# An attention + MLP block on one core: the MLP of the last chunk as its own pipeline (TensorE transposes, residual summed beforehand, w1 in two row halves, w3 in two row ranges, Newton rstd)

## The chip, the cores and the metric

The kernel runs on one core of a Trainium2 chip. The metric is device time in microseconds (us), the median of several executions.

Engine names in the profile: PE = TensorE matmul, PEld = TensorE weight load, DVE = VectorE, ACT = ScalarE, POOL = GpSimd, SPq = the DMA queue fed by SyncE.

A second measure, the **tail**: from the end of the last eviction of an attention output (the last `f_On<-f_O,f_rl`) to the end of the span, both read from the timeline of one profile. The change acts almost only there.

## The reference, cut to what matters

```python
# x: 2048 x 640; 32 heads of 128; keys and values 2048 long; w3: 640 x 1728, w4: 1728 x 640
mod = silu(c) @ w_mod                      # sa, ca, ga, sb, cb, gb: six vectors of 640
h = layernorm(x) * (1 + ca) + sa
x = x + ga * (attention(h) @ wo)           # LayerNorm without weights, eps 1e-5
h = layernorm(x) * (1 + cb) + sb
# MLP B(h):
g  = gelu(layernorm(h) @ w1)               # 640 columns in four groups of 160;
gs = shift rows of the groups by +1, -1, +2, -2
x1 = h + gs @ w2
B  = x1 + gelu(layernorm(x1) @ w3) @ w4
x = x + gb * B
```

The row shift matters: row r of `gs` needs rows r-2 to r+2 of `g`. So the MLP of the last tile of a chunk has to wait for the next chunk, and the last chunk has five tiles of 128 rows for w2, w3 and w4 instead of four.

## The kernel before: the parts that the change touches

The queries are done in four chunks of 512 rows (`NC` = 4). While attention of one chunk runs, the MLP of the chunk before it (`phase_b`) is slipped in between. The last chunk's MLP has nothing to hide behind. A small scheduler orders the operations of each engine by the priority that is the last argument of `P.op`; it then puts in semaphores for the data.

```python
    def ln(src, src_tiles, prio):                       # LayerNorm statistics and rstd
        ...                                             # 2 x bn_stats, bn_aggr on DVE
        P.op("ACT", lambda e: e.activation(rs[i].ap, mv[i][:, 1:2], ACT.Ln, bias=EPS), ...)
        P.op("ACT", lambda e: e.activation(rs[i].ap, rs[i].ap, ACT.Exp, scale=-0.5), ...)
        return mv[i], rs[i]

    def back_to_exp(g, prio):                           # EXPSET = "natural_log_exp_and_others"
        o = P.op("ACT", lambda e: e.preload_act_table_set(EXPSET), ..., after=tuple(g))
        return (o,)

    def phase_b(ch):
        last = ch == NC - 1
        ...                                             # weights w1, w2 (and once w3) by DMA
        for i in range(4):                              # residual, two LayerNorms, DMA transpose
            w = y_t * ga ; a = w + x                    # 2 DVE operations of 128x640
            mvt, rst = ln(a) ; b = modulated(a, ...)
            mvt, rst = ln(b) ; nr = (b - mean) * rstd
            dma("SP", e.dma_start_transpose(nT_t[:, :, i * 128:(i + 1) * 128], nr.ap), ...)
        for n in range(KT):                             # w1: 5 groups, each over all 512 rows
            ...matmul 128x512, then gelu into us_t, shifted by one or two columns...
        if not last:
            gate[X1 + 1, 0] = back_to_exp(g1, X1 - 2)
        for t in tl:                                    # w2: 4 tiles, in the last chunk 5
            ...matmul in two column halves, DVE adds each half into b...
            mvt, rst = ln(b) ; nr = (b - mean) * rstd   # second LayerNorm of the MLP
            dma("SP", e.dma_start_transpose(nT_t[...], nr.ap), ...)
        for f in range(NF):                             # w3: 14 groups, in the last chunk over
            for (r0, r1) in ranges:                     # two ranges of 320 rows; each reads ALL tiles
                P.op("PE", mm, KT * MM(n), (WB,) + tuple(nT[t - t0] for t in tl), (m,), ...)
                ...gelu...
        for t in tl:                                    # w4 and the output
            ...matmul in two halves; DVE: + b per half, * gb, + a; DMA out...
```

(Bodies are shortened to their arithmetic; `...` marks cuts.) Note two things: every w3 group waits for the transposes of all five tiles, and `back_to_exp`, which puts a table set with both Ln and Exp back after the gelus, is left out in the last chunk.

## Time and profile before

| | before |
|---|---|
| time, median (3 runs) | 1488.18 us (1486.7 to 1490.71) |
| span of the profiled execution | 1482.6 us |
| PE busy over the span | 94% |
| tail | 115.1 us |
| table loads on ScalarE in the tail | 12 |

The page of the kernel before: busy time and share, and the chain that ended last.

```profile
PE 1399.9 (94%) x13043; PEld 926.6 (62%) x13043; DVE 568.5 (38%) x1330; ACT 1104.1 (74%) x1292; POOL 6.2 (0%) x14
...
PE 90%; ACT 4%; DVE 3%; DMA 1%; issue 1%; SPq 0%; DVEq 0%
```

For most of the span PE is the limit, and the change does nothing about that. The busy table of the kernel before, by stretches of 20 us, shows where it is not. Columns: stretch, its length, then busy us of PE, PEld, DVE, ACT and POOL with instruction counts, the granted TensorE clock, the DMA share and GB/s.

```profile
1380.00:1400.00 20.00, 0.25 (x1) 0.13 (x2) 16.68 (x36) 4.12 (x15) 0.00 (x0) 0.50 0.15 33
1400.00:1420.00 20.00, 15.18 (x75) 6.61 (x73) 8.23 (x21) 13.35 (x20) 0.00 (x0) 0.93 0.21 57
1420.00:1440.00 20.00, 9.56 (x59) 5.68 (x60) 3.67 (x9) 12.75 (x22) 0.00 (x0) 0.74 0.25 68
1440.00:1460.00 20.00, 19.48 (x137) 11.81 (x136) 3.04 (x5) 7.60 (x18) 0.00 (x0) 1.00 0.03 9
```

PE stands almost still in 1380 to 1400 (0.25 us busy) and does half its time in 1420 to 1440. The timeline of the kernel before says why. Columns: start, duration, engine, line, operation, `out<-in`, and in brackets the idle time before it and what ended that.

```profile
1399.75 4.94 PE L578 MATMUL f_M<-f_nT,f_WA 128*128 128x512 bf16 x15 [23.38 <-DMA f_nT<-f_nrm]
...
1415.88 0.20 ACT L360 ACTIVATE f_rs<-f_mv 128x1 f32<-128x1 f32 x1 [0.29 <-DVE f_mv L359]
1416.10 1.28 ACT L361 ACT_TABLE_LOAD   x1
...
1417.40 0.20 ACT L361 ACTIVATE f_rs<-f_rs 128x1 f32<-128x1 f32 x1
1417.62 1.28 ACT L360 ACT_TABLE_LOAD   x1
1417.63 0.61 DVE L605 TENSOR_SCALAR f_nrm<-f_xb,f_mv,f_rs 128x640 bf16<-128x640 f32 x1 [0.98 <-ACT f_rs L361]
...
1427.35 0.61 DVE L605 TENSOR_SCALAR f_nrm<-f_xb,f_mv,f_rs 128x640 bf16<-128x640 f32 x1 [2.37 <-ACT f_rs L361]
...
1430.44 9.81 PE L625 MATMUL f_M<-f_nT,f_WB 128*128 128x320 bf16 x59 [10.49 <-DMA f_nT<-f_nrm]
```

w1 (L578) starts only when four tiles have been through two LayerNorms and a DMA transpose; PE had waited 23.4 us. w2's tiles then cost "Ln, table load, Exp, table load" each, 3.3 us from one normalised tile to the next, and w3 (L625) starts when the fifth is normalised and transposed: 62.9 us into the tail. From there PE is the limit: w3 21.1 us, w4 21.2 us.

### The profile page before, as it was taken

The page shows a single profiled execution, that of the slowest core. Times are in us where ns is not written, and L with a number is a line of the kernel's source. Part 1 is how long each engine was busy: PE and PEld are TensorE (multiplying, and loading weights), DVE is VectorE, ACT ScalarE, POOL GpSimd, SP SyncE. Part 2 cuts the span into 40 slices and gives each one's busy share as a digit, 9 for nine tenths or more (in the row PEclk, how much of TensorE's full clock was granted, in tenths as well). Part 3 has the DMA queues.
Part 4 walks back from the last instruction along what each step waited for, and adds up shares of the span by engine and source line. Part 5 has one row for each costly group of instructions (what it writes and reads, how often), then busy time and mean ns, then how long its engine had stood idle before and what let it go on. Part 6 is the DMA issues. An engine that isn't in the chain of part 4 may idle for free.

```text
span 1482.6 us, 30158 instructions
## 1 busy us (share of the span) xinstructions
PE 1399.9 (94%) x13043; PEld 926.6 (62%) x13043; DVE 568.5 (38%) x1330; ACT 1104.1 (74%) x1292; POOL 6.2 (0%) x14
## 2 busy tenths in 40 slices
PE   6999999999999999999999999999999999999367
PEld 3666666666666666666666566666666666666134
DVE  5332333335552135224653125322833224323633
ACT  4868888888898776788888675788888685786261
POOL 0000000000000000000000000000000000000000
PEclk8999999999999999999999999999999999999689
DMA  7997899999899478998988466988998765985020
GB/s 185 214 220 129 159 173 181 191 206 181 174 174 179 103 127 188 196 177 159 188 169 173 106 132 140 216 167 172 177 184 168 136 126 115 197 165 114 22 67 25
DMA packets 755788, 232.60 MB, mean 157 GB/s; under 512 B 716608, under 2 KB 755008, under 8 KB 755648
## 3 DMA queue, kind: packets, MB, share of 16 engines
q1 hardware_dynamic: 755648, 230.60, 78.4%
q8 instruction: 104, 1.70, 0.5%
q14 instruction: 36, 0.29, 0.1%
HBM read 136.82 MB, written 2.62 MB: 94 GB/s over the span
## 4 chain that ended last, share of the span: by engine, by line
PE 90%; ACT 4%; DVE 3%; DMA 1%; issue 1%; SPq 0%; DVEq 0%
PE f_O L475 31%; PE f_S L462 28%; PE f_M L450 9%; PE f_M L507 9%; PE f_M L646 4%; PE f_M L625 4%; ACT f_PT L465 3%; PE f_M L578 1%; PE f_M L598 1%; DVE f_st L357 1%; PE f_M L333 1%; DMA f_KTs<-in_A_k_cache_dram 1%; ACT L361 0%; DMA f_nT<-f_nrm 0%; DMA f_WA<-in_w_mod_dram 0%
## 5 line engine op out<-in xcount | busy, mean ns | idle before, releaser
L465 ACT ACTIVATE f_PT<-f_S 128x1024 bf16<-128x1024 f32 x1024 | 998.4, 1025 | 237.7 <-PE f_O L475 125.5
L475 PEld LDWEIGHTS f_O<-f_V,f_PT 128*128 128x128 bf16 x8192 | 547.6, 98 | 223.2 <-DVE f_On L486 18.9
L475 PE MATMUL f_O<-f_V,f_PT 128*128 128x129 bf16 x8192 | 640.5, 220 | 1.4 <-DVE f_On L486 0.9
L462 PE MATMUL f_S<-f_QT,f_KTs 128*128 128x512 bf16 x2048 | 603.5, 379 | 12.5 <-ACT f_PT L465 11.3
L453 DVE CAST f_QT<-f_M 128x512 bf16<-128x512 f32 x128 | 88.5, 691 | 486.0 <-PE f_M L450 485.9
L450 PE MATMUL f_M<-f_hT,f_wq 128*128 128x512 bf16 x640 | 228.6, 382 | 0.8 <-ACT f_hT L399 0.8
L462 PEld LDWEIGHTS f_S<-f_QT,f_KTs 128*128 128x128 bf16 x2048 | 165.8, 97 | 79.6 <-ACT f_PT L465 36.1
L507 PE MATMUL f_M<-f_wo,f_OT 128*128 128x320 bf16 x1024 | 179.2, 301 | 0.9 <-DVE f_yacc L515 0.8
L515 DVE TENSOR_TENSOR f_yacc<-f_M,f_yacc 128x320 f32<-128x320 f32 x224 | 109.5, 490 | 144.2 <-PE f_M L507 143.4
L507 PEld LDWEIGHTS f_M<-f_wo,f_OT 128*128 128x128 bf16 x1024 | 94.0, 98 | 61.0 <-DVE f_yacc L515 6.1
L486 DVE TENSOR_TENSOR f_On<-f_O,f_rl 128x256 bf16<-128x256 f32 x256 | 107.9, 422 | 6.6
L484 DVE RECIPROCAL f_rl<-f_O 128x2 f32<-128x2 f32 x256 | 43.4, 170 | 141.6 <-PE f_O L475 137.0
L450 PEld LDWEIGHTS f_M<-f_hT,f_wq 128*128 128x128 bf16 x640 | 62.0, 98 | 44.4 <-issue 2.2
L646 PE MATMUL f_M<-f_WA,f_gT 128*128 128x320 bf16 x448 | 79.6, 300 | 0.6 <-ACT f_gT L629 0.5
L625 PE MATMUL f_M<-f_nT,f_WB 128*128 128x512 bf16 (+5 forms) x350 | 65.9, 343 | 12.2 <-DMA f_nT<-f_nrm 10.5
L629 ACT ACTIVATE f_gT<-f_M 128x512 bf16<-128x512 f32 (+3 forms) x70 | 35.8, 511 | 39.5 <-PE f_M L625 39.4
L625 PEld LDWEIGHTS f_M<-f_nT,f_WB 128*128 128x128 bf16 (+1 forms) x350 | 31.8, 100 | 41.8 <-DMA f_nT<-f_nrm 10.8
L646 PEld LDWEIGHTS f_M<-f_WA,f_gT 128*128 128x128 bf16 x448 | 40.2, 97 | 24.8 <-issue 7.7
L578 PE MATMUL f_M<-f_nT,f_WA 128*128 128x512 bf16 x100 | 25.6, 398 | 24.7 <-DMA f_nT<-f_nrm 23.4
L360 ACT ACTIVATE f_rs<-f_mv 128x1 f32<-128x1 f32 x64 | 12.8, 203 | 41.0 <-DVE f_mv L359 40.9
L650 DVE TENSOR_TENSOR f_tmp<-f_M,f_xb 128x320 f32<-128x320 f32 x32 | 15.7, 491 | 65.9 <-PE f_M L646 65.6
L578 PEld LDWEIGHTS f_M<-f_nT,f_WA 128*128 128x128 bf16 x100 | 9.3, 101 | 36.8 <-DMA f_nT<-f_nrm 23.7
(75 smaller groups left out, 378.9 us busy)
## 6 DMA issues: line engine op xcount, KB each, us to landing
f_V<-in_A_v_cache_dram SPq DMA_DIRECT2D x128, 512.0 KB, 5.0
f_wq<-in_A_wq_dram SPq DMA_DIRECT2D x128, 160.0 KB, 2.9
f_wo<-in_A_wo_dram SPq DMA_DIRECT2D x32, 640.0 KB, 5.0
f_WA<-in_B_w_dram SPq DMA_DIRECT2D x40, 160.0 KB, 2.9
f_WA<-in_B_w_dram SPq DMA_DIRECT2D x8, 800.0 KB, 5.1
f_xin<-in_A_x_dram SPq DMA_DIRECT2D x32, 160.0 KB, 3.6
out_dram<-f_ob SPq DMA_DIRECT2D x16, 160.0 KB, 4.0
f_WA<-in_w_mod_dram SPq DMA_DIRECT2D x3, 800.0 KB, 5.3
```

The lines of the kernel that those rows point to most:

```text
L450: P.op("PE", lambda e, kk=kk: e.matmul(m.ap, w[:, kk, :], hT_t[ch % 2][:, kk, :], start=(kk == 0), stop=(kk == KT - 1)), MM(QC), (w,) + tu ...
L453: P.op("DVE", lambda e: e.tensor_copy(q.ap, m.ap), dve(QC, True), (m,), (q,), s - 4)
L462: ins = e.matmul(sp[:, r * QC:(r + 1) * QC], k[:, kt * 128:(kt + 1) * 128], q.ap, start=True, stop=True)
L465: last_exp[s, j] = P.op("ACT", lambda e, sp=sp, pt=pt: e.activation(pt.ap.rearrange("p k q -> p (k q)"), sp.ap, ACT.Exp, scale=SCALE), 104 ...
L475: ins = e.matmul(o[b][:, u * 129:u * 129 + 129], pt[:, r, qt * 128:(qt + 1) * 128], v[:, kt, 0:129], start=(kt == 0 and u == 0), stop=(kt ...
L484: P.op("DVE", lambda e, ov=ov, i0=i0: e.reciprocal(rl_t[:, i0:i0 + 2].unsqueeze(2), ov[:, 0:258].rearrange("p (u d) -> p u d", u=2)[:, :, ...
L486: P.op("DVE", lambda e, ov=ov, i0=i0, b=b: e.tensor_tensor(out=On_t[gs][:, 2 * b:2 * b + 2, hh, :], in0=ov[:, 0:258].rearrange("p (u d) -> ...
L507: ins = e.matmul(m[:, 0:HD], OT_t[gs][:, qt, hh, :], w[:, hh, sl], start=(hh == 0), stop=(hh == HG - 1))
L515: P.op("DVE", lambda e, m=m, qt=qt, sl=sl: e.tensor_tensor(out=y_t[:, qt, sl], in0=m[:, 0:HD], in1=y_t[:, qt, sl], op=ALU.add), dve(HD, Tr ...
L578: ins = e.matmul(m.ap, w1v[:, kk, n * 128:(n + 1) * 128], nT_t[:, kk, 0:QC], start=(kk == 0), stop=(kk == KT - 1))
L625: ins = e.matmul(m[0:fs[f], 0:n], w3v[:, kk, f * 128:f * 128 + fs[f]], nT_t[:, kk, r0:r1], start=(kk == 0), stop=(kk == KT - 1))
L646: ins = e.matmul(m[:, 0:HD], gT_t[0:fs[f], f, i * 128:(i + 1) * 128], w4v[0:fs[f], f, sl], start=(f == 0), stop=(f == NF - 1))
```

## The change

The intent: give the last chunk its own code, in which each stage starts on the first tiles as soon as they are there, and take waiting and detours out of the chain. In short:

- the last `wo` group goes straight from PSUM to the residual, on TensorE-transposed attention outputs; ga times the sum of the earlier groups, plus x, is formed on GpSimd beforehand (`tail_front`);
- the `wo` matmuls of the last but one group pulled closer together (priority steps of 0.2 instead of 0.5; not in the cut below), so that their sum is ready for that;
- all transposes of the tail on TensorE, copied out of PSUM by ScalarE;
- w1 in two halves of 256 rows, w3 in two row ranges (tiles 0 and 1, tiles 2 to 4), each waiting only for its own tiles;
- the rstd of the second LayerNorm by three Newton steps (seed on VectorE, nine GpSimd operations of 128x1) instead of Ln and Exp, so that no table load is needed there;
- gb times b plus x1 formed on GpSimd while w3 runs, so the output needs two VectorE operations per tile instead of four.

```diff
-        if not last:
-            gate[X1 + 1, 0] = back_to_exp(g1, X1 - 2)
+        gate[X1 + 1, 0] = back_to_exp(g1, X1 - 2)
 ...
+    def pe_transpose(src, n, reads, dst, dst_t, prio):      # n PE transposes into one PSUM tile,
+        ...                                                 # then one ScalarE copy
+    def rstd_newton(v, i, prio):
+        r, q = rs[i], nw[i]
+        P.op("DVE", ... q0 = var + EPS)
+        P.op("DVE", ... r = q0 as int >> 1)
+        P.op("DVE", ... r = 0x5f3759df - r, as int)
+        for _ in range(3):
+            P.op("POOL", ... q1 = r * r * q0)               # tensor_scalar, 128x1
+            P.op("POOL", ... q1 = 1.5 - 0.5 * q1)           # tensor_scalar, 128x1
+            P.op("POOL", ... r = r * q1)                    # tensor_tensor, 128x1
+    def tail_front(ch):                                     # queued 4 heads before the end
+        for i in range(4):
+            P.op("POOL", ... y = y * ga) ; P.op("POOL", ... y = y + x)
+    def tail(ch):
+        for i in range(4):
+            pe_transpose(On...) ; wo: 8 matmuls
+            P.op("DVE", ... v = wo * ga) ; P.op("DVE", ... a = v + y)
+            mvt, rst = ln(a) ; modulated(...) ; mvt, rst = ln(b) ; nr = ...   # Ln and Exp as before
+            pe_transpose(nr...)
+        for hv in range(2):                                 # w1, rows 0-255, then 256-511
+            ...matmul 128x256 needs nT[2*hv], nT[2*hv+1]; gelu...
+        for i in range(5):                                  # w2
+            ...matmul; P.op("DVE", ... b = w2 + b); bn; rstd_newton; nr = ...; pe_transpose(nr...)
+            P.op("POOL", ... b = b * gb, priority pr + 5)
+            P.op("POOL", ... b = b + a,  priority pr + 5)
+        for i0, i1 in ((0, 2), (2, 5)):                     # w3 over tiles 0-1, then tiles 2-4
+            for f in range(NF):
+                ...matmul needs nT[i0:i1] alone; gelu...
+        for i in range(5):                                  # w4
+            ...P.op("DVE", ... v = w4 * gb) ; P.op("DVE", ... o = v + b) ; DMA out
 ...
-        phase_b(ch)
+        if ch < NC - 1:
+            phase_b(ch)
+        else:
+            tail(ch)
```

(The added arithmetic is written as formulas. In the list of added lines `i` is the tile.)

## The prediction

> **What bounds it now.** The page: span 1482.6 us, PE busy 94%; the chain of waits is 90% PE. That holds until attention ends near 1367 us. The last chunk's MLP then runs alone, and the busy table by stretches shows it: PE is busy 0.25 us of 1380–1400, 15.2 of 1400–1420, 9.6 of 1420–1440, 19.5 of 1440–1460. So the tail, about 115 us, is bounded by stages in turn (timeline): 1367–1397 VectorE (residual, two LayerNorms, four tiles); 1397–1399.7 a DMA transpose; 1400–1408.6 w1; 1408.7–1430.4 w2 with five times "Ln, table load, Exp, table load" (3.3 us a tile, each load 1.28) and another DMA transpose (2.4 us in the chain); 1430.4–1473.2 w3 and w4, PE-bound (21.1 us each); then output. Before 1367 nothing is on offer.
>
> **What the change does.** The order of instructions before the last two wo groups is unchanged. In the tail:
> - Removed: 8 VectorE adds of wo into yacc (0.49 us each, 3.9), most DMA transposes (2.4 us each; PE 0.7 cold plus ScalarE copy 0.69 instead), two table loads of twelve, Ln/Exp of the second LayerNorm.
> - Added: Newton rstd, 3 VectorE and 9 GpSimd operations on 128x1 per tile. The trace has no such GpSimd operation; I estimate 0.2 us each (its 128x32 memset is 0.13), so 3.6 us for two interleaved tiles. GpSimd also takes 128x640 f32 multiply and add. The Trainium skill, "GPSIMD Engine Reference", section 3.1, gives 4497 ns for a 2048-element tensor_tensor; scaled, an estimate of 1.4 us. No run here shows it yet.
> - Moved: w1 in two halves. But in ScalarE's new order the Ln/Exp pairs of tiles 2 and 3 sit between the gelus of half 0: three times load, Ln, load, Exp, load (about 4.3 us each, 13 in all). VectorE's normalisation of tiles 2 and 3 waits for them. The skill, "ScalarE: Activation LUTs", section "What ACT_TABLE_LOAD costs", says about 1283 ns a load; the trace agrees (1283), without the further drain.
>
> **Sum, walked by hand with the trace's durations.** Tiles 0 and 1 normalised at 1383; half 0 of w1 gelu'd at 1401, not 1391, because of the table loads; half 1 at 1411.7 (before: all of w1 at 1408.6, so this stage loses 3 us). w2, Newton and transposes overlap it, so w3's first range starts near 1417.5 instead of 1430.4: 13 us gained. From there PE is nearly continuous: 256-column groups paced by the two PSUM banks (0.6 us each, 14), 2 inserted transposes 1.5, w4 4.2 us a tile, 384-column groups 0.82 each: PE ends near 1460.5 instead of 1473.2. The last output saves 0.5 (no half add). Gain 13 us, 0.9%.
>
> **Prediction: 1475 us, range 1466 to 1482** (8 in 10). Faster by over 2%: 3%; within 2%: 96%; slower by over 2%: 1%.
>
> **What would show it right.** Timeline: w1's gelus stretched over 1386–1412 with about ten table loads among them; VectorE idle 3 to 10 us for ScalarE's rstd of tiles 2 and 3; first w3 matmul at 1415–1420; then PE over 90% busy; start of tail within 1 us of 1367.
>
> **What would make it wrong.** GpSimd's small operations at 0.4 us or its 640-wide ones at 2.5: PE would stall at the transposes of the last three tiles, and 5 to 9 us go back. A first w3 matmul before 1412 would mean the table loads hid better than I think: 1466 or less. Cold PE clock through w3: 2 us more.

## The result, and the profile after

| | before | after |
|---|---|---|
| time, median (4 runs each, same rounds) | 1487.44 us (1485.82 to 1490.71) | 1478.95 us (1478.29 to 1479.21) |
| ratio | | 0.994, 95% interval 0.9922 to 0.9957 |
| span of the profiled execution | 1482.6 | 1477.0 |
| tail | 115.1 | 104.2 |
| first w3 matmul, us into the tail | 62.9 | 50.0 |
| table loads in the tail | 12 | 10 |

A ratio is the mean time of one kernel's fast runs over that of the other's fast runs of the same rounds, so it is not quite the ratio of the medians. The verdict is "same" at 2%, as predicted: 0.6% faster, where the prediction had 0.9%.

**Two profiles cannot be laid over each other by absolute time.** These are the last attention evictions of before and of after, from which the tail is counted:

```profile
1367.10 0.42 DVE L486 TENSOR_TENSOR f_On<-f_O,f_rl 128x256 bf16<-128x256 f32 x1
```

```profile
1372.36 0.42 DVE L490 TENSOR_TENSOR f_On<-f_O,f_rl 128x256 bf16<-128x256 f32 x1
```

After's tail starts 5.3 us later. Of that, 4.4 us were already there at head 124 of 128, before the first instruction that differs, and they had built up over the whole span. It is noise of the execution: over the profiles of after and of its eleven variants, all of which leave this prefix alone, the start of head 124 lies anywhere from 1321.0 to 1327.9 us, with the same instructions before it (but for matmul records missing from some traces). From head 124 to the last eviction, however, it is 46.6 us in all of them and 45.8 us in before, 0.84 us less. The likely cause is the wo matmuls that were pulled together: in after, head 126, in which they now stand, takes 2.7 us longer, and head 127 takes 1.8 less. No run undoes this part alone. So the reproducible gain is 10.8 us of tail (115.06 less 104.23) less 0.8, which is 10.0 us; the medians show 8.5.

The busy table of the kernel after, same columns (its tail starts at 1372.8):

```profile
1380.00:1400.00 20.00, 5.67 (x28) 3.02 (x29) 15.51 (x33) 10.63 (x22) 0.00 (x0) 0.55 0.00 0
1400.00:1420.00 20.00, 13.71 (x89) 8.21 (x87) 7.24 (x19) 15.16 (x25) 5.40 (x19) 0.76 0.14 40
1420.00:1440.00 20.00, 16.51 (x133) 11.12 (x134) 9.53 (x27) 7.70 (x18) 17.77 (x36) 1.00 0.14 44
1440.00:1460.00 20.00, 19.42 (x123) 11.09 (x120) 2.96 (x3) 7.12 (x15) 2.49 (x2) 1.00 0.05 17
```

In 1420 to 1440 PE now does 16.5 us instead of 9.6, and GpSimd, idle in the tail before, is busy 17.8 of 20 us. The timeline of the kernel after, in two places:

```profile
1394.34 1.28 ACT L364 ACT_TABLE_LOAD   x1
...
1395.64 0.20 ACT L364 ACTIVATE f_rs<-f_mv 128x1 f32<-128x1 f32 x1
1395.86 1.28 ACT L365 ACT_TABLE_LOAD   x1
1397.15 0.20 ACT L365 ACTIVATE f_rs<-f_rs 128x1 f32<-128x1 f32 x1
1397.37 1.28 ACT L752 ACT_TABLE_LOAD   x1
1397.46 0.89 DVE L383 SCALAR_TENSOR_TENSOR f_xb<-f_tmp,f_rs,f_mod 128x640 f32<-128x640 f32 x1 [3.82 <-ACT f_rs L365]
...
1418.78 1.54 POOL L780 TENSOR_TENSOR f_xb<-f_xb,f_mod 128x640 f32<-128x640 f32 x1
1418.87 1.80 DVE L776 TENSOR_SCALAR f_nrm<-f_xb,f_mv,f_rs 128x640 bf16<-128x640 f32 x1 [0.80 <-POOL f_rs L697]
...
1422.83 5.49 PE L790 MATMUL f_M<-f_nT,f_WB 128*128 128x256 bf16 x45
...
1429.13 0.44 PE L677 MATMUL f_M<-f_ident,f_nrm 128*128 128x128 bf16 x5 [0.81 <-DVE f_nw L687]
```

First, the table loads: in the middle of w1's gelus stands load, Ln, load, Exp, load, 4.3 us, for one rstd of tile 2, and VectorE waits 3.8 us for it (L383). Second, from 1418 on GpSimd paces: the normalisation at 1418.87 took 1.80 us where the same operation takes 0.61, beside a GpSimd operation of 1.54; and the transposes that w3's first range has to let through (L677) wait for VectorE. The chain that ended last, in order of time, of the kernel after:

```profile
1418.87 1.82 DVE f_nrm L776
...
1420.75 1.55 POOL f_xb L780
1422.30 2.72 POOL f_xb L781 x2
...
1433.48 1.49 POOL f_xb L780
1434.97 0.15 POOL f_rs L697
1435.12 1.36 POOL f_xb L781
```

The small Newton result (L697, 0.15 us) stands in GpSimd's queue between residual operations of 1.4 to 1.5 us each (L780, L781), and the chain runs through both.

The tail's sum closes: w3 starts 12.9 us sooner (62.9 to 50.0); from there to the end of w4 it takes 45.7 us instead of 42.8, so 2.9 are lost; the output after the last matmul is 0.9 shorter (8.5 instead of 9.4). 12.9 - 2.9 + 0.9 = 10.9, but for rounding the 10.8 above.

### The profile page after: what moved, and what is told of

Read it like the earlier page. It is cut to its first block, busy times and chain, and to the rows that moved or that the text cites. A ratio compares the mean times of both kernels' runs of the same rounds, so it can differ in the third digit from the quotient of the medians.

```text
span 1477.0 us, 30150 instructions
## 1 busy us (share of the span) xinstructions
PE 1393.4 (94%) x12903; PEld 933.0 (63%) x13129; DVE 563.7 (38%) x1322; ACT 1109.9 (75%) x1302; POOL 43.3 (3%) x77
## 4 chain that ended last, share of the span: by engine, by line
PE 84%; ACT 6%; DMA 3%; DVE 3%; issue 2%; POOL 1%; SPq 1%
PE f_O L479 30%; PE f_S L466 27%; PE f_M L514 9%; PE f_M L454 8%; ACT f_PT L469 4%; PE f_M L661 3%; PE f_M L641 3%; DMA f_KTs<-in_A_k_cache_dram 2%; PE f_S L807 1%; PE f_M L620 1%; PE f_M L601 1%; DMA f_V<-in_A_v_cache_dram 1%; PE f_M L790 1%; PE f_M L333 1%; DVE f_st L356 0%
## 5 line engine op out<-in xcount | busy, mean ns | idle before, releaser
L466 PE MATMUL f_S<-f_QT,f_KTs 128*128 128x512 bf16 x1876 | 566.6, 379 | 26.1 <-ACT f_PT L469 13.7
L454 PE MATMUL f_M<-f_hT,f_wq 128*128 128x512 bf16 x592 | 210.5, 382 | 0.9 <-ACT f_hT L403 0.8
L514 PE MATMUL f_M<-f_wo,f_OT 128*128 128x320 bf16 x992 | 173.0, 299 | 0.2
L661 PE MATMUL f_M<-f_WA,f_gT 128*128 128x320 bf16 (+1 forms) x308 | 58.4, 299 | 0.2
L641 PE MATMUL f_M<-f_nT,f_WB 128*128 128x512 bf16 (+3 forms) x208 | 44.7, 362 | 2.0 <-ACT f_gT L645 1.7
L645 ACT ACTIVATE f_gT<-f_M 128x512 bf16<-128x512 f32 (+3 forms) x42 | 23.6, 562 | 28.2 <-PE f_M L641 28.2
L661 PEld LDWEIGHTS f_M<-f_WA,f_gT 128*128 128x128 bf16 (+1 forms) x308 | 27.4, 97 | 15.9 <-issue 5.1
L641 PEld LDWEIGHTS f_M<-f_nT,f_WB 128*128 128x128 bf16 (+1 forms) x210 | 19.3, 98 | 22.7 <-ACT f_gT L645 5.6
L356 DVE BATCH_NORM_STATS2 f_st<-f_xb 128x6 f32<-128x320 f32 x64 | 29.9, 484 | 0.4
L605 ACT ACTIVATE f_us<-f_M 32x512 bf16<-32x512 f32 (+3 forms) x27 | 16.0, 594 | 9.3 <-PE f_M L601 9.1
L665 DVE TENSOR_TENSOR f_tmp<-f_M,f_xb 128x320 f32<-128x320 f32 x22 | 10.8, 492 | 31.6 <-PE f_M L661 31.3
```

Of the source, the lines that this page charges most:

```text
L356: P.op("DVE", lambda e, hf=hf: e.bn_stats(st[i][:, hf * 6:hf * 6 + 6], src[:, hf * HD:(hf + 1) * HD]), dve(HD), src_tiles, (st[i],), prio)
L454: P.op("PE", lambda e, kk=kk: e.matmul(m.ap, w[:, kk, :], hT_t[ch % 2][:, kk, :], start=(kk == 0), stop=(kk == KT - 1)), MM(QC), (w,) + tu ...
L466: ins = e.matmul(sp[:, r * QC:(r + 1) * QC], k[:, kt * 128:(kt + 1) * 128], q.ap, start=True, stop=True)
L514: ins = e.matmul(m[:, 0:HD], OT_t[gs][:, qt, hh, :], w[:, hh, sl], start=(hh == 0), stop=(hh == HG - 1))
L641: ins = e.matmul(m[0:fs[f], 0:n], w3v[:, kk, f * 128:f * 128 + fs[f]], nT_t[:, kk, r0:r1], start=(kk == 0), stop=(kk == KT - 1))
L661: ins = e.matmul(m[:, 0:HD], gT_t[0:fs[f], f, i * 128:(i + 1) * 128], w4v[0:fs[f], f, sl], start=(f == 0), stop=(f == NF - 1))
```

## The experiments

Each kernel is the changed kernel (in one case the kernel before) with the edit shown. All results were correct. For each: what was expected, and what it gave. Rows with the same letter under "chip" ran on the same chip beside the same runs of before.

| kernel | chip | time, us (median) | ratio to before | tail | w3 starts | w4 starts | last tile normalised | table loads |
|---|---|---|---|---|---|---|---|---|
| before | | | 1 | 115.1 | 62.9 | 84.5 | 60.4 | 12 |
| after | | 1478.95 | 0.994 | 104.2 | 50.0 | 61.9 | 66.2 | 10 |
| e1: w1 whole | a | 1481.97 | 0.9958 | 106.9 | 52.0 | 66.2 | 64.0 | 1 |
| e2: gelus behind the last Exp | a | 1481.29 | 0.9957 | 106.2 | 51.5 | 65.3 | 62.5 | 1 |
| e3: Ln and Exp again | a | 1506.47 | 1.0127 | 127.9 | 60.5 | 87.3 | 79.5 | 29 |
| e4: transposes by DMA | a | 1476.58 | 0.9923 | 102.4 | 50.8 | 59.9 | 66.4 | 9 |
| e5: residual on VectorE | b | 1476.73 | 0.9925 | 102.8 | 49.5 | 59.9 | 65.0 | 10 |
| e6: e2 and e5 together | b | 1478.62 | 0.994 | 105.2 | 49.2 | 64.4 | 61.6 | 1 |
| e7: w3 row ranges undone | b | 1491.81 | 1.0036 | 119.0 | 67.8 | 89.8 | 66.2 | 10 |
| e8: before, with Newton alone | b | 1490.73 | 1.0021 | 119.5 | 66.7 | 88.4 | 64.0 | 1 |
| e9: Newton on VectorE | c | 1476.46 | 0.9916 | 101.4 | 49.2 | 59.3 | 61.6 | 10 |
| e10: e2 and e9 together | c | 1473.76 | 0.9905 | 99.6 | 47.8 | 57.4 | 60.0 | 1 |
| e11: e10, second transposes by DMA | c | 1479.17 | 0.9938 | 105.5 | 52.1 | 63.6 | 60.3 | 1 |
| e12: e10, residual in another order | d | 1472.27 | 0.9913 | 99.5 | 47.9 | 57.5 | 58.7 | 1 |

The columns from "tail" on are from one profile each, so a difference of a few tenths in them is not read; stages are in us from the start of the tail. 95% intervals of the ratios are 0.0013 to 0.0026 either way. Before's median on the chips a to d was 1488.32, 1487.21, 1487.99 and 1486.17.

### First question: what are the table loads between w1's gelus worth?

**e1, w1 in one pass of 512 columns.** Then the gelus can't start before tile 3, and no Ln or Exp falls between them.

```diff
-        for hv in range(2):
-            c0 = hv * 256
-            for n in range(KT):
-                ...matmul m[:, 0:256] needs nT[2 * hv:2 * hv + 2]...
+        for n in range(KT):
+            ...matmul m.ap, 512 columns, needs nT[0:4]...
```

> One part undone: w1 of the last chunk again in one 512-column pass instead of two 256-column halves; all else as in the changed kernel. Measure: the tail, from the end of the last attention-output eviction (On) to the end of the span; 104.2 us in the changed kernel, 115.1 before; first w3 matmul 50.0 us into the tail. Theory A (halving w1 costs, because Ln/Exp of tiles 2 and 3 then sit between gelus, with ten table loads; what gains is the rest): the eight Ln/Exp pairs come first, two table loads instead of ten, first w3 matmul at 44 to 47 us, tail 3 to 6 us SHORTER than the changed kernel's. Theory B (the overlap of the two w1 halves carries the gain): tail 4 or more us LONGER, first w3 matmul after 54 us.

Measured: tail 106.9, 2.7 us longer, with 1 table load instead of 10. The gelus are all done at 36.4 us instead of 43.3, and yet w3 starts 2.0 us later. Neither number was met: the halves are worth keeping, but less than the wait for tile 3 suggests (against e2 below, which has halves and the same single load, 0.7 us of tail), and getting rid of nine loads (11.5 us of ScalarE) brought nothing to the start of w3.

**e2, halves kept, every gelu behind the last Exp.** The early PE start stays, the loads go.

```diff
-        P.op("ACT", ... Exp ...)
+        exps.append(P.op("ACT", ... Exp ...))
 ...
-                        ... gelu of w1 ..., base + 2 + hv)
+                        ... gelu of w1 ..., base + 2 + hv, after=tuple(exps[-2:]))
```

> Changed kernel with one added rule of order: no gelu of w1 before the last Exp of the first four tiles' LayerNorms; halves kept. Theory A: two table loads instead of ten in the w1 stage; VectorE no longer waits 3 to 5 us each for rstd of tiles 2 and 3; half 0 of w1 done at about 29 us into the tail instead of 33.5, first w3 matmul at 43 to 46 us instead of 50.0; tail 97 to 100 us instead of 104.2. Theory B (the table loads are hidden behind other waits; the GpSimd chain of the second LayerNorm sets the start of w3): tail within 1.5 us of 104.2.

Measured: tail 106.2, 2.0 us longer. Loads 1, gelus done at 37.4 instead of 43.3, w2's matmuls done at 42.2 instead of 50.2, and w3 starts at 51.5 instead of 50.0. Eight microseconds gained at w2 vanish before w3. The timeline of e2 shows where (L694, L696 and L698 are Newton's three operations, L781 and L782 the residual):

```profile
1415.57 1.54 POOL L781 TENSOR_TENSOR f_xb<-f_xb,f_mod 128x640 f32<-128x640 f32 x1 [0.73 <-DVE f_rs L689]
1417.10 0.34 POOL L694 TENSOR_SCALAR f_nw<-f_rs,f_nw 128x1 f32<-128x1 f32 x1
1417.40 1.40 POOL L782 TENSOR_TENSOR f_xb<-f_xb,f_x 128x640 f32<-128x640 f32 x1
1418.76 0.19 POOL L696 TENSOR_SCALAR f_nw<-f_nw 128x1 f32<-128x1 f32 x1
...
1422.39 0.72 PE L678 MATMUL f_M<-f_ident,f_nrm 128*128 128x128 bf16 x5 [6.38 <-DVE f_rs L691]
```

The residual operations of tile 0 stand before and between the Newton steps of tile 1 in GpSimd's queue, and PE is idle 6.4 us before it can transpose tile 1. So the theory that the loads are simply on the path fell. A new one was needed: GpSimd paces the second LayerNorm (theory C in what follows).

The traces show a second loss that the theories left out. In e2 the TensorE clock granted fell to 0.50 during that idle time and stayed there until 56.6 us into the tail, so w3's first 5 us ran at half the clock; in after it was 1.00 from 36.6 on. The rows of the busy table, of e2 and then of after, over the first microseconds of w3 (the third figure from the end is the clock):

```profile
1423.90:1428.80 4.90, 4.90 (x26) 3.44 (x27) 0.46 (x3) 1.84 (x4) 4.90 (x14) 0.50 0.00 0
```

```profile
1422.80:1428.30 5.50, 5.50 (x47) 3.73 (x44) 3.57 (x15) 3.07 (x8) 5.14 (x15) 1.00 0.49 150
```

PE is busy throughout in both, but does 26 matmuls and transposes in 4.9 us in e2 and 47 in 5.5 us in after. At half the clock for 5 us, some 2.5 us are lost (an estimate), about as much as w3's first range grew: start of w3 to start of w4 takes 13.8 us in e2 and 11.8 in after. The same holds of e1 (0.50 until 56.5), e6 (until 54.0) and e11 (until 57.8), but not of e4, e5, e9, e10 and e12 (1.00 from the start of w3). Before, e7, e8 and e3, where PE also waits long, have a low clock in w3 too (before until 66.0). So a wait before w3 is paid for twice in these kernels.

### Second question: what was the Newton rstd worth?

**e3, Ln and Exp again in the second LayerNorm.**

```diff
-            n_st[0] += 1
-            bn(b.ap, (b,), k, pr)
-            rstd_newton(mv[k], k, pr)
+            ln(b.ap, (b,), pr)
```

> One part undone: the second LayerNorm of the tail gets rstd from ScalarE's Ln and Exp again instead of Newton steps; all else as in the changed kernel. Theory A (table loads on ScalarE are what this tail is sensitive to): twenty or more table loads in the tail, the order has gelus of half 1 between them; tail 8 to 15 us longer than 104.2, so about as long as before's 115 or longer. Theory B (the Newton chain of nine dependent GpSimd operations is as slow as the table loads it replaces): tail within 2 us of 104.2.

Measured: tail 127.9, 23.7 us longer, 29 table loads instead of 10. The direction was expected, the size not. Ln and Exp of five tiles now interleave with gelus one by one. Timeline of e3:

```profile
1420.38 1.28 ACT L364 ACT_TABLE_LOAD   x1
1421.68 0.20 ACT L364 ACTIVATE f_rs<-f_mv 128x1 f32<-128x1 f32 x1
1421.90 1.28 ACT L752 ACT_TABLE_LOAD   x1
1423.19 0.38 ACT L752 ACTIVATE f_us<-f_M 64x256 bf16<-64x256 f32 x1
```

**e8, the kernel before with Newton alone.** If Newton is worth 23.7 us in one kernel, what is it worth in the other?

```diff
-            mvt, rst = ln(b.ap, (b,), pr)
+            mvt, rst = (ln_newton if last else ln)(b.ap, (b,), pr)
```

> The kernel before with one part of the change alone: Newton rstd (on VectorE and GpSimd) for the last chunk's second LayerNorm instead of Ln and Exp. Before: 12 table loads in the tail, tail 115.1. If the table loads of that LayerNorm are what before's tail loses: loads drop to 3 or 4, the last tile is normalised 5 to 7 us sooner, tail 108 to 110, time about 1482. If VectorE paces that stage in before anyway, or Newton's chain is no shorter than the loads: tail 113 to 116, time within 1.5 of before.

Measured: table loads 12 to 1, and the tail is 4.4 us *longer*: 119.5. The direction is the second theory's, but it had allowed only 116. In before, ScalarE had nothing else to do in that stage, and its "Ln, load, Exp, load" of 3.3 us a tile went beside VectorE. Newton's nine dependent GpSimd operations take 2.9 us a tile, plus the seed, and the last tile is normalised at 64.0 instead of 60.4. So Newton is no gain in itself. It is what makes the pipeline possible: with w1's halves and w3's ranges, gelus and rstds want ScalarE at the same time, and only then do the loads explode.

### Third question: what turned the earlier tiles into time?

**e7, w3's row ranges undone.** All else is kept; w3 over two ranges of 320 rows that need all five tiles.

```diff
-        for i0, i1 in ((0, 2), (2, 5)):
-            r0, r1 = i0 * 128, i1 * 128
-            for f in range(NF):
+        for f in range(NF):
+            for r0, r1 in ((0, 320), (320, 640)):
-                ... (WB,) + tuple(nT[i0:i1]) ...
+                ... (WB,) + tuple(nT) ...
```

> The changed kernel with w3 over two 320-row ranges that both need all five normalised tiles, as before the change; all else kept. If the row ranges are what turns an earlier start into time, as the prediction said: w3 can only start when the last tile is normalised and transposed, 62 to 67 us after the last eviction (before: 62.9), w3 itself then takes about 21 us as before, and the tail is 112 to 117, that is 8 to 13 us longer and no better than before's 115.1. Rival (the gain comes from the summed residual and Newton wherever w3 starts): tail 106 to 108.

Measured: tail 119.0, 14.7 us longer and 3.9 us longer than before's. The direction is that of the first theory, the size beyond its range, and w3 starts at 67.8, after a last tile normalised at 66.2, later than in before (60.4). This is the plainest statement of what the change does: it normalises its *last* tile 5.8 us later than before and its first two only 2.1 and 2.8 us sooner (45.3 and 47.9 instead of 47.4 and 50.7), and the row ranges let w3 start on those two. The ranges, more than the sooner tiles, make the 12.9 us. The row ranges put into the kernel before, without the rest, were not tried; e3 suggests that Ln and Exp among w3's gelus would have taken the gain back.

### Fourth question: does GpSimd pace, and by what?

**e4, all 13 transposes of the tail by DMA.** Meant as the undoing of one part.

```diff
     def pe_transpose(src, n, reads, dst, dst_t, prio):
-        ...PE transposes, then a ScalarE copy...
+        dma("SP", lambda e: e.dma_start_transpose(dst, src), 40 * n, tuple(reads), (dst_t,), prio, dur=1250)
```

> One part undone: the tail's thirteen transposes go by DMA again (2.4 us from issue to landing in the chain before) instead of TensorE plus a ScalarE copy (0.45 to 0.71 plus 0.69 us). Theory A (transposes overlap other stages except about four that end a wait: attention output of tile 0, nT of tile 1, and the last tiles of the second LayerNorm): tail 2 to 6 us longer than 104.2. Rival C (TensorE transposes carry most of the gain of 11 us): tail 8 or more us longer.

Measured: tail 102.4, 1.9 us *shorter*; both theories had the sign wrong. w1 starts 2.5 us later (19.6 instead of 17.1 us into the tail), as one would think. But w3's first range goes through in one piece. Timeline of e4:

```profile
1422.37 8.56 PE L782 MATMUL f_M<-f_nT,f_WB 128*128 128x256 bf16 x70 [0.32 <-DMA f_nT<-f_nrm]
```

70 matmuls in 8.56 us; in after the same 70, with transposes of tiles 2 and 3 in PE's queue among them, took 11.3 us. Of the 2.8 us more, PE waited 1.4 for the two tiles (0.8 and 0.6) and 0.5 behind the ScalarE copies, and the transposes themselves took 0.9. The transposes in PE's queue held up the matmuls behind them until the tile was ready; the DMA transposes waited in another queue.

**e5, the residual operations on VectorE.**

```diff
-            P.op("POOL", ... b = b * gb ...) ; P.op("POOL", ... b = b + a ...)
+            P.op("DVE",  ... b = b * gb ...) ; P.op("DVE",  ... b = b + a ...)
```

> The changed kernel with the ten 640-wide residual operations of the second LayerNorm's tiles (times gb, plus x1) on VectorE instead of GpSimd; Newton's small operations stay on GpSimd. Tail = from the end of the last attention-output eviction to the end of the span; 104.2 us in the changed kernel. Theory C (GpSimd's in-order queue, filled with Newton and ten 1.4 to 1.5 us residual operations, delays the rstd of tiles 2 to 4 and so starves w3's first row range): w3 starts at 50 after that eviction as now, its first range takes 9 to 10 us instead of 11.3, the last tile is normalised by 62 instead of 66, tail 101 to 102.5, time about 1476 to 1477. Rival (the first range is slow because of the transposes and their ScalarE copies themselves, whatever feeds them): first range stays at 11 us or more, tail 104.2 plus or minus 0.7.

Measured: tail 102.8, 1.5 us shorter: between the two, nearer to theory C. w3's first range (start of w3 to start of w4) goes from 11.8 to 10.4. The last tile, expected by 62, is normalised at 65.0.

**e6, the gate of e2 with the residual on VectorE** (both diffs together).

> The gelus of w1 kept behind the last Exp (the experiment of the first call, tail 106.2) and also the residual operations on VectorE. Theory C: with the GpSimd queue free, the 6 us that the gelus gained reach w3: it starts at 45 to 46.5 after the last eviction instead of 50.0, tail 97 to 100, time 1471 to 1475, about 3 us better than the residual move alone. Rival (the table loads never were worth anything, since some other chain such as VectorE's normalising paces w3): w3 starts at 49 or later, tail 102 or more, no better than the residual move alone.

Measured: tail 105.2, w3 starts at 49.2, no better than the residual move alone. The rival's numbers, all of them. The loss lies in w3's first range, 15.3 us against e5's 10.4, and has two parts that the theories did not have: the clock stood at 0.50 until 54.0 (4.8 us, some 2.4 lost by the same estimate as in e2), and in this order of PE's queue the *fifth* tile's transpose, too, stands in the first range: PE waits 1.9 us for it at 61.7. In e1 and e2 that transpose stands there as well (waits of 0.3 and 0.5 us). With table loads and residual both out of the way, GpSimd still paces the tiles. Timeline of e6, normalised tiles and, below, one Newton operation with its neighbour on VectorE:

```profile
1415.15 0.61 DVE L777 TENSOR_SCALAR f_nrm<-f_xb,f_mv,f_rs 128x640 bf16<-128x640 f32 x1 [1.34 <-POOL f_rs L698]
1419.32 0.61 DVE L777 TENSOR_SCALAR f_nrm<-f_xb,f_mv,f_rs 128x640 bf16<-128x640 f32 x1 [1.19 <-POOL f_rs L698]
1423.05 0.61 DVE L777 TENSOR_SCALAR f_nrm<-f_xb,f_mv,f_rs 128x640 bf16<-128x640 f32 x1 [1.26 <-POOL f_rs L698]
...
1428.37 1.55 DVE L781 TENSOR_TENSOR f_xb<-f_xb,f_mod 128x640 f32<-128x640 f32 x2
1428.55 2.15 POOL L694 TENSOR_SCALAR f_nw<-f_rs,f_nw 128x1 f32<-128x1 f32 x1 [0.81 <-DVE f_rs L691]
```

Each normalisation waited for GpSimd's last Newton operation, and the next tile's seed stands behind it in VectorE's queue, so the chain of one tile can't overlap that of the next: 4.2 and 3.7 us between these tiles. That is latency, not work. And the Newton operation at 1428.55 took 2.15 us instead of 0.34: it outlasted a row of three two-input 128x640 operations on VectorE, the two shown and a third (L782) that ends at 1430.65, and ended 0.05 us after the third.

**e9, Newton's nine operations on VectorE**, residual back on GpSimd.

```diff
         for _ in range(3):
-            P.op("POOL", ...) ; P.op("POOL", ...) ; P.op("POOL", ...)
+            P.op("DVE", ...)  ; P.op("DVE", ...)  ; P.op("DVE", ...)
```

> The changed kernel with Newton's nine small operations per tile on VectorE, straight behind their seed, instead of GpSimd; residual operations back on GpSimd, table loads as in the changed kernel (10). Theory D (what paces the second LayerNorm, once the table loads are out of the way, is the latency of Newton's nine dependent GpSimd operations, 2.9 to 3.0 us per tile, with VectorE's in-order queue standing behind each): here tiles 0 and 1 still wait for the gelus of w1, so w3 starts only 0 to 1.5 us sooner (48.5 to 50 after the last eviction) and the tail is 101.5 to 103.5 against 104.2. Rival (VectorE has no room: 45 more operations of about 0.14 us are 6 us more on the engine that normalises): tail 104.5 to 107.

Measured: tail 101.4, 2.9 us shorter, w3 at 49.2. Tail just below, start within theory D's range; the rival (no room on VectorE) fell, though VectorE is the engine that normalises. The last tile is normalised at 61.6 instead of 66.2.

**e10, the gate of e2 with Newton on VectorE** (both diffs together).

> The gelus of w1 behind the last Exp (tail 106.2 alone, 105.2 with the residual on VectorE) with Newton's operations on VectorE, residual on GpSimd. Theory D: the two together remove both paces, w3 starts 44 to 47 after the last eviction instead of 51.5, the tiles are normalised every 2 to 2.5 us instead of every 4, tail 98 to 101, time 1472 to 1475. Rival (the gate itself costs: with all gelus late, w2 and the normalising are bunched and PE idles, whatever computes the rstd): w3 starts at 49 or later, tail 104 or more.

Measured: tail 99.6, 4.7 us shorter than after. The tail is within theory D's range. The start of w3, 47.8, lies between the theories: better than the rival's 49, not the 44 to 47 that I wrote. The gate, worth -2.0 us with Newton on GpSimd, is worth +1.8 with Newton on VectorE (101.4 to 99.6). So e2's answer was right for its kernel and wrong as a general one: the loads did cost time, and another wait, with the low clock that followed it, hid it. In e10 PE waits 1.9 us before tile 0's transpose, and the clock is back at 1.00 before w3 starts. But the spacing of the tiles did not come down to 2 to 2.5 us; it is still 3.8 to 5.3, and the timeline of e10 shows one cause:

```profile
1416.18 0.14 DVE L696 TENSOR_SCALAR f_nw<-f_nw 128x1 f32<-128x1 f32 x1
...
1416.58 1.40 POOL L782 TENSOR_TENSOR f_xb<-f_xb,f_x 128x640 f32<-128x640 f32 x1
1416.63 1.37 DVE L698 TENSOR_TENSOR f_rs<-f_rs,f_nw 128x1 f32<-128x1 f32 x1
```

A VectorE multiply of 128x1 that takes 0.15 us elsewhere took 1.37 and ended within 0.02 us of GpSimd's residual operation. Other operations (L694, L696, bn_stats) run at their usual time beside GpSimd. The Trainium skill, "SBUF — State Buffer", section "SBUF: two separate sides", describes this: VectorE and GpSimd share one port pair as an exclusive lock, which a GpSimd operation takes, and a VectorE operation with two SBUF inputs (against a GpSimd operation that reads SBUF, as all here do) or in a two-port mode; "the other fully blocks". The trace agrees: the loser waited to the end, in both directions (2.15 us on GpSimd in e6, 1.37 and, for the normalisation, 1.80 on VectorE; that the normalisation, with its one wide input, ran in a two-port mode is not shown).

**e11, e10 with the second LayerNorm's transposes by DMA**, to collect what e4 had shown.

```diff
-            pe_transpose(nr.ap, KT, (nr,), nT_t[:, :, i * 128:(i + 1) * 128], nT[i], pr)
+            dma("SP", ... e.dma_start_transpose(nT_t[:, :, i * 128:(i + 1) * 128], nr.ap) ..., pr, dur=1250)
```

> As the run before it, with the five tiles of the second LayerNorm transposed by DMA as before the change (the first LayerNorm's stay on TensorE). All 13 transposes by DMA gave a tail of 102.4 against 104.2: 2.5 us lost at the start of w1, 2.7 us and more won in w3's first row range, from which five transposes and their ScalarE copies had gone. If the two add to the gate and Newton on VectorE: w3's first range takes 8.6 to 9 us without breaks, the tail is 1 to 3 us shorter than in the run before it (95 to 100). If the DMA's 2.3 to 2.6 us per tile comes into the chain before w3 instead: w3 starts 1 to 2 us later and the tail is the same within 1 us or longer.

Measured: tail 105.5, 6.0 us longer. The second theory's direction; w3 starts 4.2 us later where it had said 1 to 2, and its first range, now without a transpose in it, still takes 11.5 us. Timeline of e11:

```profile
1424.14 11.03 PE L791 MATMUL f_M<-f_nT,f_WB 128*128 128x256 bf16 x70 [5.52 <-DMA f_nT<-f_nrm]
```

Tile 1 was normalised at 1418.9 and its transpose landed at 1424.1: 5.0 us instead of the usual 2.6 from issue to landing. A load of w4 had been issued 0.4 us ahead of it. That the load delayed the transpose is likely, but I did not test it. PE was idle 5.5 us meanwhile, and the clock was 0.50 until 57.8 us into the tail: the same 70 matmuls that took 8.56 us in e4, at clock 1.00, took 11.03. So this run does not show what DMA transposes would be worth without the slow landing.

**e12, e10 with the residual operations meant to run after the last tile's normalisation.**

```diff
-            P.op("POOL", ... b = b * gb ..., pr + 5) ; P.op("POOL", ... b = b + a ..., pr + 5)
+        for i in range(5):      # behind the loop, ordered after the last normalisation
+            P.op("POOL", ... b = b * gb ..., base + 8.5 + 0.5 * i, after=(nop,))
+            P.op("POOL", ... b = b + a ...,  base + 8.5 + 0.5 * i, after=(nop,))
```

> The fastest run so far (gelus behind the last Exp, Newton on VectorE: tail 99.5) with the ten 640-wide residual operations left on GpSimd but queued behind the last tile's normalising, so that none of them runs while VectorE computes rstd. In that run VectorE's 128x1 tensor_tensor took 0.15 us alone and 1.37, 0.95, 1.37, 0.66 and 0.94 us where a GpSimd residual operation was under way, each ending with it. If the two engines exclude each other there (theory E), those five stretched operations go back to 0.15 us: w3 starts about 1.2 us sooner (46.5 after the last eviction instead of 47.8), the last tile is normalised at 55 to 57 instead of 60.0, tail 97.5 to 99, time 1471 to 1473.5. If the stretched operations wait for something else (the Newton chain itself), they stay over 0.6 us with GpSimd idle, and the tail is 99 to 101.

Measured: tail 99.5, as e10's 99.6, and **the edit did not do what I meant**. `after` only sets the order in which the scheduler places operations; across engines it puts in no semaphore, and as GpSimd had nothing else to do, the first residual operation ran at once behind the first tile. All that changed is GpSimd's order (multiply, multiply, add, add). The repeat has two uses. It shows how well the tail reproduces: 99.55 and 99.48 us. And by the changed order the very instruction shown above no longer met a GpSimd operation, while another one did. Timeline of e12:

```profile
1412.19 0.14 DVE L698 TENSOR_TENSOR f_rs<-f_rs,f_nw 128x1 f32<-128x1 f32 x1
...
1414.57 2.75 POOL L784 TENSOR_TENSOR f_xb<-f_xb,f_x 128x640 f32<-128x640 f32 x2
...
1415.17 0.82 DVE L698 TENSOR_TENSOR f_rs<-f_rs,f_nw 128x1 f32<-128x1 f32 x1
```

The first line is the same instruction as e10's 1.37 us, in both some 44.5 us into the tail: 0.14 with GpSimd idle. The last one took 0.82 and ended at 1415.99, where the first of the two GpSimd adds ends if it takes the usual 1.40. So it is shown that the stretched time comes and goes with GpSimd's operation; that taking the overlap away altogether would shorten the tail is not: in e12 the second tile was normalised 1.1 us sooner and w3 started no sooner.

**The version that beats both.** e10 and e12 are the same but for that order. Against before on their own chips they gave 0.9905 (0.988 to 0.9931) and 0.9913 (0.9899 to 0.9926), where after gave 0.994 (0.9922 to 0.9957). The intervals overlap a little, so the ratios alone do not show that they beat after; the tails, 99.6 and 99.5 against 104.2, do. About 0.9% better than before by the ratios (14 us between the medians), and some 4.7 us better than after by the tail.

## Why the prediction was right

Predicted 1475.0 us (1466 to 1482, within 2%); measured 1478.95. The range held. Point by point, with after's profile shifted back by the 5.3 us by which its tail began later than before's:

| step of the prediction | predicted | measured |
|---|---|---|
| tiles 0 and 1 normalised | 1383 | 1383.0 |
| half 0 of w1 gelu'd | 1401 | 1401.0 |
| half 1 of w1 gelu'd | 1411.7 | 1410.9 |
| first w3 matmul | 1417.5 | 1417.6 |
| PE ends | 1460.5 | 1463.3 |
| table loads in the tail | two fewer of 12 | 10 |
| VectorE's waits for rstd of tiles 2 and 3 | 3 to 10 us | 3.8, 5.3 and 4.0 |
| 640-wide GpSimd operation | 1.4 us (estimate) | 1.40 (add), 1.54 (multiply) |
| Newton operation on GpSimd | 0.2 us (estimate) | 0.34, 0.19, 0.19, with gaps 2.9 for nine |
| PE busy from the first w3 matmul to its end | over 90% | 93% |
| tail starts | within 1 us of 1367 | 1372.8, not shifted |

- **Right: what was on offer.** The first w3 matmul, in the frame of the tail, came within 0.1 us of the walk by hand. The order of each engine was known beforehand and most durations were in before's trace. That it came so close is in part luck: the chain to it holds tile 1's normalisation, stretched by 1.2 us beside a GpSimd operation, which the prediction did not have, and half 1 of w1 was done 0.8 us sooner than predicted.
- **Right: the table loads between w1's gelus, and when its two halves are done.** They took the place predicted (three times load, Ln, load, Exp, load; in the third the last load comes 2 us late). e10 against e9 shows that an order without them gains 1.8 us once nothing else hides it. In after itself, removing them gains nothing (e1, e2). The prediction took them for the limit of that stage and did not see the second one behind it.
- **Mis-sized: "From there PE is nearly continuous".** This is the term that failed, though PE was over 90% busy, as predicted. The prediction allowed 9.9 us for w3's first range (14 times 0.6, and 1.5 for two transposes); to the start of w4 it took 11.8, and the second range took 12.2 instead of 11.5. Together with smaller terms PE ends 2.8 us late. The groups themselves were sized right (e4: 8.56 us for 14), and so were the transposes with the waits behind their copies (1.4); what was left out is 1.4 us in which PE waits for the tiles. The cause: the transposes of tiles 2 and 3 stand in PE's queue and wait for GpSimd, where Newton's chain (2.9 us alone) and residual operations of 1.4 to 1.5 us take turns. The prediction had named this danger but for operations of 2.5 us (640 wide) or 0.4 (small); at 1.4 to 1.5 and 0.19 to 0.34 the queue was already too long. The other danger it named, a low clock through w3, did not come in after; it came in e1, e2, e6 and e11. e4, e5 and e9 each take a part of it away and gain 1.9, 1.5 and 2.9 us.
- **Missed: the shared port.** A normalisation of 0.61 us took 1.80. It lies before w3's start, not in the term above.
- **Missed: attention's end**, 0.84 us later, probably because the last but one wo group's matmuls moved.
- **Wrong as written: "start of tail within 1 us of 1367".** It was off by 5.8 us, of which 4.4 are the noise of an execution. A signature in absolute time was a bad one; it should have been given from a common instruction on.

What the sum gave: 13 us predicted; 10.8 in the tail, 10.0 with attention's end, 8.5 between the medians. The last 1.5 us, between the profile's account and the medians, I leave to the spread of the executions (before's profiled run was, at 1484.27 us, the fastest of its runs). What remains open: the value of the residual summed beforehand was not tried by itself, nor were the row ranges in the kernel before; and why w3's second range took 0.7 us more than predicted and what made the landing in e11 slow was not followed up.

A further way was seen and not tried. In before's last chunk each rstd after the gelus pays two table loads, because `back_to_exp` is left out there. Wherever that set was in place, Ln and Exp started 0.24 us apart with no load, as the first LayerNorms of e10 do (one load in the whole tail, for the gelus). Putting the set back after w1's gelus might have spared the kernel before most of these loads without Newton. That is a guess from the traces, not a result.

## What to carry to other kernels

Value a part of a pipeline by undoing it in the finished version, not by adding it to the old one: Newton alone made the old kernel 4 us slower and its absence makes the new one 24 us slower, and the gate on the gelus changed sign with the engine that computes the rstd. A dependent chain of nine tiny operations is a latency of some 3 us on GpSimd, and it paces whatever follows if the consumer's in-order queue stands behind it; here it did best on the engine that needs the result (e9, e10), with the wide operations out of that engine's queue. Look at the granted clock beside every wait of PE: here four kernels that let PE wait 3.7 to 6.4 us shortly before w3 (e1, e2, e6, e11) also ran w3's first 4.5 to 5.7 us at half the clock. Compare two profiles from the last instruction that they have in common, not in absolute time.

## What the Trainium skill lacked or had wrong

- "ScalarE: Activation LUTs", section "What ACT_TABLE_LOAD costs", adds a drain of about 1380 ns to each load. Here each load took 1.28 us and the next activation followed 0.02 us later (1416.10 to 1417.40 in before); no drain is seen.
- The same page, "Table sets: the hidden batching unit", has Ln followed by Exp at one load, since one set holds both. That held only where the kernel had put that set in place explicitly; after gelus, the loads that were put in automatically were one for each Ln and one for each Exp: 10 loads for five tiles in before, and 29 in the tail of e3, those for gelus among them.
- "GPSIMD Engine Reference", section 3.1, compares wide operations only. Its 4497 ns at 2048 columns, scaled to 640, is an estimate of 1.41 us and fits the 1.40 and 1.54 measured. It has nothing on 128x1 operations in a dependent chain: 0.34, 0.19 and 0.19 us, 2.9 us for nine with the gaps, where VectorE's take 0.14 to 0.15 (0.27 with two scalars).
- "SBUF — State Buffer", section "SBUF: two separate sides", has the exclusive lock right, but gives no size for short operations: a 128x1 multiply on VectorE went from 0.15 to 1.37 us beside one GpSimd operation, and a 128x1 GpSimd operation from 0.34 to 2.15, beside not one but three VectorE operations in a row.
- No page that I read draws from the order of PE's queue that a PE transpose in it stalls the matmuls behind it where a DMA transpose does not: 11.3 against 8.56 us for the same 70 matmuls, 1.4 of it waiting for the tiles.
